# The softmax's 1e-9 added on GpSimd instead of VectorE, and two pairs of one-element VectorE operations joined

## The chip, the cores and the metric

One core of a Trainium2 chip runs the whole kernel. The metric is the device time of one execution in microseconds (us); smaller is better. In the profile PE is TensorE, DVE is VectorE, ACT is ScalarE, POOL is GpSimd and SP is SyncE.

## What is computed

A window attention with global tokens (4 batches, 8 heads, 512 local and 32 global positions, 64 elements a head, all float32), and behind it two feed-forward networks on the 2,176 rows that come out.

```python
def sm(s):
    s = s - np.max(s, axis=-1, keepdims=True)
    e = np.exp(s)
    return e / (np.sum(e, axis=-1, keepdims=True) + 1e-09)
out_g = sm(q_g @ [k_g, k_l].T / 8) @ [v_g, v_l]           # each global query sees all 544 keys
out_l = sm([q_l @ k_g.T / 8, where(|i-j|<=32, q_l @ k_l.T / 8, -1e9)]) @ [v_g, v_l]
x = (x @ w_in) * cos(x @ w_in) @ w_out                    # first network, 512 -> 2048 -> 512
y = relu(x @ w2_in)**2 @ w2_out                           # second network
```

## The kernel before

The attention is cut into 40 items. A **local item** is half of the queries of a pair of heads: four units `u`, each of 128 rows of scores with 160 keys (128 of the window, 32 global). There are 32 of them, numbered 0 to 31 here in the order in which they run. After each four local items comes a **global item** (8 in all), in which 128 rows of global queries see 544 keys.

The items run as a software pipeline. At step `s` a fixed list of stages (`CFG['order']`) is written out, each for the item that is `lag` steps behind; every engine works through its own instructions strictly in the order in which they are written, and waits at an instruction until what it needs is there. The stages that matter here, in the order of one step:

- `S`: PE computes the scores into PSUM (L400, for a global item L526).
- `KC`: POOL copies parts of the transposed keys (L333, L335, L343).
- `CC`: POOL finishes a piece of a weight's conversion (L163). `BG` and `CB` are more such background work for the networks, put on POOL, DVE or ACT by a table of room per step: L142, L172, L185, L724 on POOL, L151, L156, L172, L185, L724 on DVE.
- `SM` (item s): for each unit DVE adds the mask and finds the maximum (L416, two rows each in the profile); ACT takes the exponential and sums the row (L426). For a global item DVE finds two maxima (L541), joins them (L546), scales by -0.125 (L547), and ACT takes the exponentials (L551).
- `RC` (item s-1): DVE adds 1e-9 to the four sums in the small tile `st` (L440), then takes the reciprocal (L443). For a global item DVE adds two sums (L565), adds 1e-9 (L568), takes the reciprocal (L571).
- `NM` (item s-1): POOL scales the global-key part into `pg` (L448) and units 1 to 3 (L455); DVE scales unit 0 (L455). For a global item POOL scales all of `ptg` (L575).
- `OE`: DVE or ACT copies a finished output out of PSUM (L509, L613).
- `TM`, `TE`, `OM` in later steps: PE transposes the scaled weights (L468, L469; L583 for a global item), ACT copies them (L474, L478), PE multiplies with the values (L484, L496, L602).

Behind the attention come the steps of the two networks, ordered by a planner; their first matmuls (L850) stand in PE's queue between the last of the attention. The planner has nothing to do with the stages above.

Of the kernel before, what the change touches and what calls it, by code (L numbers as in the profile page):

```python
# [16 lines left out]
ALU = mybir.AluOpType  # L17
# [35 lines left out]
def kernel(  # L53
# [14 lines left out]
    nc = tc.nc  # L68
# [319 lines left out]
    class Local:  # L388
# [20 lines left out]
        def softmax(self):  # L409
            self.pt = lp.tile([P, 4, KTB], F32, tag="pt", name="pt", bufs=4)  # L410
            self.st = lp.tile([P, 3, 4], F32, tag="st", name="st", bufs=4)

            def unit(u):
                i = 2 * self.hb + u % 2
                m = masks[1] if i == 0 else masks[2] if i == 3 else masks[0]
                nc.vector.tensor_tensor_reduce(  # L416
                    out=self.pt[:, u, :],
                    in0=self.s[u // 2][:, 160 * (u % 2) : 160 * (u % 2) + 160],
                    in1=m,
                    scale=-0.125,  # L420
                    scalar=3.0e38,
                    op0=ALU.add,
                    op1=ALU.min,
                    accum_out=self.st[:, 0, u : u + 1],
                )
                nc.scalar.activation(  # L426
                    self.pt[:, u, :],
                    self.pt[:, u, :],
                    AF.Exp,
                    bias=self.st[:, 0, u : u + 1],  # L430
                    scale=-1.0,
                    accum_out=self.st[:, 1, u : u + 1],
                )

            return [lambda u=u: unit(u) for u in range(4)]

        def recip(self):
            st = self.st
            return [
                lambda: nc.vector.tensor_scalar(  # L440
                    st[:, 2, :], st[:, 1, :], 1e-9, None, op0=ALU.add
                ),
                lambda: nc.vector.reciprocal(st[:, 2, :], st[:, 2, :]),  # L443
            ]
# [69 lines left out]
    class Global:  # L514
# [19 lines left out]
        def softmax(self):  # L534
            self.pt = lp.tile([P, 544], F32, tag="ptg", name="ptg", bufs=1)
            self.st = lp.tile([P, 8], F32, tag="stg", name="stg", bufs=2)
            st = self.st
            n = (320, 224)

            def top(i):  # L540
                nc.vector.tensor_reduce(  # L541
                    st[:, i : i + 1], self.s[i][:, 0 : n[i]], op=ALU.max, axis=AX.X
                )

            def rest():
                nc.vector.tensor_tensor(st[:, 2:3], st[:, 0:1], st[:, 1:2], op=ALU.max)  # L546
                nc.vector.tensor_scalar(  # L547
                    st[:, 2:3], st[:, 2:3], -0.125, None, op0=ALU.mult
                )
                for i in range(2):  # L550
                    nc.scalar.activation(  # L551
                        self.pt[:, 320 * i : 320 * i + n[i]],
                        self.s[i][:, 0 : n[i]],
                        AF.Exp,
                        bias=st[:, 2:3],
                        scale=0.125,
                        accum_out=st[:, 4 + i : 5 + i],
                    )

            return [lambda: top(0), lambda: top(1), rest]  # L560

        def recip(self):
            st = self.st
            return [
                lambda: nc.vector.tensor_tensor(  # L565
                    st[:, 6:7], st[:, 4:5], st[:, 5:6], op=ALU.add
                ),
                lambda: nc.vector.tensor_scalar(  # L568
                    st[:, 6:7], st[:, 6:7], 1e-9, None, op0=ALU.add
                ),  # L570
                lambda: nc.vector.reciprocal(st[:, 6:7], st[:, 6:7]),  # L571
            ]
# [903 lines left out]
```

## Time and profile before

| | |
|---|---|
| time, median of 3 runs | 875.22 us (874.52 to 875.74) |
| time of the profiled execution | 873.37 us, its span 871.5 us |
| busy share of the span | PE 98%, DVE 75%, ACT 61%, POOL 67% |
| attention, and networks behind it | to about 148 us; from there to the end |

The profiled execution's own time is 1.9 us above its span, and 1.85 us below the median of the runs. A busy share is a mean over stages that differ: in the attention four engines are nearly full, behind it PE is. The profile counts an instruction as busy from its start to its end, also while it is held up inside; what an engine waits for ahead of an instruction is shown as idle time.

### The profile page before, as it was taken

The numbers are of one execution on the slowest core, as the hardware profiler recorded it, in microseconds if no ns is written. First come the engines' busy times: TensorE is split into PE (matmuls) and PEld (weight loads), VectorE is DVE, ScalarE is ACT, GpSimd is POOL, SyncE is SP. The second block draws the span as 40 slices with busy tenths as digits, with TensorE's granted clock in tenths as the row PEclk, the third lists the DMA queues.
The fourth block names the chain that finished last, engine by engine and source line by source line (L and its number), as shares of the span: only waits on it lengthen the run. The fifth ranks groups of instructions, "written<-read, shape, count | busy, mean of one in ns | idle before, by whom it ended". The sixth has DMA issues, their size and how long they took to land.

```text
span 871.5 us, 17134 instructions
## 1 busy us (share of the span) xinstructions
PE 849.9 (98%) x6028; PEld 783.9 (90%) x6028; DVE 656.7 (75%) x1409; ACT 531.5 (61%) x1275; POOL 583.5 (67%) x666
## 2 busy tenths in 40 slices
PE   7889999999999999999999999999999999999998
PEld 5668777999999999999999998889888989898886
DVE  6589997899798777967788898896756767454544
ACT  5679887987776656666555867655544554342331
POOL 6479998899887564758358899985645647432221
PEclk9999999999999999999999999999999999999999
DMA  7899664547774577557727547566764687346633
GB/s 164 201 205 206 136 209 140 229 177 252 286 291 176 192 303 271 168 171 302 278 73 260 216 171 266 195 229 235 276 209 141 242 297 222 131 166 248 214 119 85
DMA packets 134261, 182.00 MB, mean 209 GB/s; under 512 B 60960, under 2 KB 114720, under 8 KB 134176
## 3 DMA queue, kind: packets, MB, share of 16 engines
q1 hardware_dynamic: 130736, 179.79, 62.6%
q10 hardware_dynamic: 3440, 1.11, 0.5%
q8 instruction: 48, 0.79, 0.4%
q14 instruction: 37, 0.30, 0.1%
HBM read 141.03 MB, written 35.65 MB: 203 GB/s over the span
## 4 chain that ended last, share of the span: by engine, by line
PE 82%; DVE 6%; POOL 4%; ACT 2%; DMA 2%; issue 1%; SPq 1%; POOLq 0%; ACTq 0%
PE y L942 41%; PE hb L850 16%; PE ha L850 10%; PE he L850 10%; DVE pt L416 1%; POOL xs L172 1%; ACT pt L426 1%; PE s L400 1%; PE o L484 1%; POOL g L172 1%; DMA kn<-in_k_l_dram 1%; PE o L496 1%; POOL xr L724 1%; PE og L602 1%; POOL wf L163 1%
## 5 line engine op out<-in xcount | busy, mean ns | idle before, releaser
L172 POOL TENSOR_TENSOR g<-cr,g 128x384 fp32r<-128x384 f32 (+1 forms) x192 | 203.8, 1074 | 144.9 <-ACT g L901 139.4
L953 DVE TENSOR_TENSOR xt<-y,xt 128x384 f32<-128x384 f32 (+2 forms) x287 | 170.5, 596 | 96.2 <-PE y L942 94.5
L942 PE MATMUL y<-g,wo 128*128 128x384 f32 (+1 forms) x1152 | 219.1, 327 | 0.5 <-DVE xt L953 0.4
L942 PE MATMUL y<-wo,g 128*128 128x512 f32 x816 | 209.4, 393 | 0.0
L942 PEld LDWEIGHTS y<-g,wo 128*128 128x128 f32 x1152 | 193.9, 188 | 1.6 <-ACT wo L205 0.7
L942 PEld LDWEIGHTS y<-wo,g 128*128 128x128 f32 x816 | 150.0, 188 | 24.1
L850 PE MATMUL hb<-xs,wi 128*128 128x384 f32 (+1 forms) x864 | 167.3, 328 | 1.4 <-ACT cr L890 1.2
L850 PEld LDWEIGHTS hb<-xs,wi 128*128 128x128 f32 x864 | 147.7, 189 | 7.6 <-ACT cr L890 1.6
L850 PE MATMUL he<-xs,wi 128*128 128x384 f32 (+1 forms) x576 | 111.4, 328 | 1.4 <-DVE he L864 0.8
L850 PE MATMUL ha<-xs,wi 128*128 128x384 f32 (+1 forms) x576 | 111.2, 328 | 0.5 <-ACT ptg L551 0.5
L901 ACT ACTIVATE g<-cr 128x384 fp32r<-128x384 f32 (+1 forms) x192 | 93.9, 502 | 20.3 <-DVE cr L893 19.4
L163 POOL TENSOR_TENSOR wf<-wf,cc 128x512 uint32<-128x512 uint32 x64 | 87.8, 1376 | 24.9 <-DVE wf L151 18.2
L850 PEld LDWEIGHTS he<-xs,wi 128*128 128x128 f32 x576 | 98.2, 188 | 5.9 <-DVE cr L893 1.2
L850 PEld LDWEIGHTS ha<-xs,wi 128*128 128x128 f32 x576 | 97.9, 188 | 3.3 <-ACT ptg L551 0.8
L887 ACT ACTIVATE cr<-cr,halfpi 128x384 f32<-128x384 f32 (+1 forms) x96 | 56.0, 594 | 9.9 <-DVE cr L882 8.6
L156 DVE SCALAR_TENSOR_TENSOR cc<-raw,cc 128x512 uint32<-128x512 uint32 x64 | 61.9, 973 | 0.0
L426 ACT ACTIVATE pt<-pt,st 128x160 f32<-128x160 f32 x128 | 53.2, 423 | 2.7 <-DVE st L416 2.4
L147 ACT ACTIVATE cc<-raw 128x512 uint32<-128x512 uint32 x64 | 42.4, 670 | 20.3 <-DMA raw<-in_moe_w_out_dram 9.0
L151 DVE TENSOR_SCALAR wf<-wf 128x512 uint32<-128x512 uint32 x64 | 49.3, 775 | 4.3 <-POOL wf L142 3.2
L858 ACT ACTIVATE s<-hb 128x384 f32<-128x384 f32 (+1 forms) x48 | 22.7, 473 | 48.8 <-PE hb L850 48.7
L858 ACT ACTIVATE s<-he 128x384 f32<-128x384 f32 (+1 forms) x48 | 22.6, 472 | 32.5 <-PE he L850 32.4
L172 POOL TENSOR_TENSOR wi<-ws,wi 128x512 fp32r<-128x512 f32 x23 | 30.8, 1342 | 15.9 <-ACT wi L196 12.3
(147 smaller groups left out, 1338.4 us busy)
## 6 DMA issues: line engine op xcount, KB each, us to landing
xs<-xs_T SPq DMA_DIRECT2D x48, 768.0 KB, 5.9
xs<-xs_B SPq DMA_DIRECT2D x36, 768.0 KB, 5.5
raw<-in_moe_w_in_dram SPq DMA_DIRECT2D x32, 512.0 KB, 5.3
raw<-in_moe_w_out_dram SPq DMA_DIRECT2D x32, 512.0 KB, 4.5
xs<-xs_T SPq DMA_DIRECT2D x24, 640.0 KB, 5.5
xs_T<-xs SPq DMA_DIRECT2D x16, 768.0 KB, 4.3
xs<-xs_B SPq DMA_DIRECT2D x18, 640.0 KB, 5.3
xs_B<-xs SPq DMA_DIRECT2D x12, 768.0 KB, 4.9
```

The costliest lines, as they stand in the source:

```text
L147: A.activation(v, raw[q, m, c][:, :, 0].bitcast(U32), AF.Copy, scale=2.0**-29)
L151: V.tensor_scalar(u, u, 3, None, op0=ALU.logical_shift_left)
L156: V.scalar_tensor_tensor(v, t[:, :, 1].bitcast(U32), 0x80000000, v, op0=ALU.bitwise_and, op1=ALU.bitwise_or,)
L163: G.tensor_tensor(u, u, v, op=ALU.add)
L172: eng.tensor_tensor(lo, x, hi.bitcast(F32), op=ALU.subtract)
L426: nc.scalar.activation(self.pt[:, u, :], self.pt[:, u, :], AF.Exp, bias=self.st[:, 0, u : u + 1], scale=-1.0, accum_out=self.st[:, 1, u : ...
L850: nc.tensor.matmul(out, lhsT=w[:, ws, c : c + P], rhs=xs[:, xh, kk, 0:n], start=start and k == 0, stop=k == 5, skip_group_check=True,)
L858: A.activation(self.sb[name], self.hold(bank_name), AF.Copy)
L887: A.activation(self.r[key], self.r[key], AF.Sin, bias=halfpi, scale=TWOPI)
L901: A.activation(GT[s, f][0][:, th * n : th * n + n], self.r[key], AF.Copy)
L942: nc.tensor.matmul(o, lhsT=l, rhs=r, start=k == 0, stop=k == 5)
L953: V.tensor_tensor(dst, y, dst, op=ALU.add)
```

## The change

The 1e-9 of the 32 local items goes from a DVE instruction to a POOL instruction on the same four numbers per partition; the reciprocal stays on DVE. In the 8 global items the maximum and the factor become one DVE instruction, and so do the sum and the 1e-9. What is computed stays the same.

```diff
         def recip(self):                       # local item
             st = self.st
             return [
-                lambda: nc.vector.tensor_scalar(
-                    st[:, 2, :], st[:, 1, :], 1e-9, None, op0=ALU.add
+                lambda: nc.gpsimd.tensor_scalar(
+                    st[:, 2, :], st[:, 1, :], 1e-9, 1.0, op0=ALU.add, op1=ALU.mult
                 ),
                 lambda: nc.vector.reciprocal(st[:, 2, :], st[:, 2, :]),
             ]
             def rest():                        # global item, softmax
-                nc.vector.tensor_tensor(st[:, 2:3], st[:, 0:1], st[:, 1:2], op=ALU.max)
                 nc.vector.tensor_scalar(
-                    st[:, 2:3], st[:, 2:3], -0.125, None, op0=ALU.mult
+                    st[:, 2:3], st[:, 0:1], st[:, 1:2], -0.125, op0=ALU.max, op1=ALU.mult
                 )
         def recip(self):                       # global item
             return [
-                lambda: nc.vector.tensor_tensor(
-                    st[:, 6:7], st[:, 4:5], st[:, 5:6], op=ALU.add
-                ),
                 lambda: nc.vector.tensor_scalar(
-                    st[:, 6:7], st[:, 6:7], 1e-9, None, op0=ALU.add
+                    st[:, 6:7], st[:, 4:5], st[:, 5:6], 1e-9, op0=ALU.add, op1=ALU.add
                 ),
                 lambda: nc.vector.reciprocal(st[:, 6:7], st[:, 6:7]),
             ]
```

How it moves instructions is seen in each engine's order. First DVE's, where a global item's softmax meets a local item's reciprocal (`stg` and `sg` belong to the global item, `st` and `pt` to the local one; behind each row the engines that it waits for). Before:

```order
L541 TENSOR_REDUCE stg<-sg 128x1 [waits PE_49] x2
L546 TENSOR_TENSOR stg<-stg 128x1 [waits DVE_49]
L547 TENSOR_SCALAR stg<-stg 128x1 [waits DVE_49]
L440 TENSOR_SCALAR st<-st 128x4 [waits Activation_49]
L443 RECIPROCAL st<-st 128x4 [waits DVE_49]
L455 TENSOR_SCALAR pt<-pt,st 128x128 [waits DVE_49]
L509 COPY xt<-o 128x256 [waits PE_49]
```

And in the changed kernel, at the same place:

```order
L541 TENSOR_REDUCE stg<-sg 128x1 [waits PE_49] x2
L546 TENSOR_SCALAR stg<-stg 128x1 [waits DVE_49]
L443 RECIPROCAL st<-st 128x4 [waits Pool_49]
L455 TENSOR_SCALAR pt<-pt,st 128x128 [waits DVE_49,Activation_49]
L509 COPY xt<-o 128x256 [waits PE_49]
```

Two rows are gone, and the reciprocal L443, which waited for DVE's own add, now waits for POOL.

Then POOL's queue from the key copies of one step to the scaling of local item 19 (`wf` and `cc` are background work on a weight). Before:

```order
L343 TENSOR_SCALAR kT<-ktail 128x64
L163 TENSOR_TENSOR wf_1569<-wf_1569,cc 128x512 [waits DVE_49]
L448 TENSOR_TENSOR pg<-pt,st 128x128 [waits PE_49,DVE_49,Activation_49,Pool_49]
L455 TENSOR_SCALAR pt<-pt,st 128x128 x3
L142 TENSOR_SCALAR wf_1569<-raw 128x512 [waits DMAHW1_49]
L448 TENSOR_TENSOR pg<-pt,st 128x128 [waits PE_49,DVE_49,Activation_49,Pool_49]
L455 TENSOR_SCALAR pt<-pt,st 128x128 x3
```

And in the changed kernel:

```order
L343 TENSOR_SCALAR kT<-ktail 128x64
L163 TENSOR_TENSOR wf_1561<-wf_1561,cc 128x512 [waits DVE_49]
L440 TENSOR_SCALAR st<-st 128x4 [waits Activation_49]
L448 TENSOR_TENSOR pg<-pt,st 128x128 [waits DVE_49,PE_49]
L455 TENSOR_SCALAR pt<-pt,st 128x128 x3
L142 TENSOR_SCALAR wf_1561<-raw 128x512 [waits DMAHW1_49]
L440 TENSOR_SCALAR st<-st 128x4 [waits Activation_49]
L448 TENSOR_TENSOR pg<-pt,st 128x128 [waits DVE_49,PE_49]
L455 TENSOR_SCALAR pt<-pt,st 128x128 x3
```

The add L440 stands directly ahead of the item's first scaling L448, behind all the copies and background work that POOL has ahead of it; L448 still waits for DVE, whose reciprocal now waits for L440. The orders of PE, ACT and SP are the same as before. In the changed kernel's file the lines behind L546 have numbers that are lower by 1 to 4.

## Rows read from the trace of the kernel before

**Rows 1.** The page's list of busy time: us, share of the span, instructions.

```profile
PE 849.9 (98%) x6028; PEld 783.9 (90%) x6028; DVE 656.7 (75%) x1409; ACT 531.5 (61%) x1275; POOL 583.5 (67%) x666
```

**Rows 2.** Busy time by stretch: stretch, its length, then each engine, TensorE's granted clock.

```profile
66.90:141.70 74.80, 72.43 (x1157) 57.83 (x1156) 71.76 (x292) 66.86 (x244) 68.92 (x130) 1.00 0.65 162
141.70:148.60 6.90, 6.39 (x76) 5.67 (x75) 4.54 (x11) 3.74 (x9) 6.90 (x9) 1.00 0.85 305
148.60:871.00 722.40, 715.41 (x4030) 675.86 (x4028) 533.97 (x898) 416.67 (x859) 465.70 (x432) 1.00 0.61 215
```

**Rows 3.** Two long pieces of the chain of waits, 74 to 125 us: start, duration.

```profile
75.81 1.06 DVE st L440
...
90.15 1.27 POOL wf L163
```

**Rows 4.** POOL's groups of instructions, 66.9 to 141.7: busy, mean | idle before, released by.

```profile
L455 POOL TENSOR_SCALAR pt<-pt,st 128x128 f32<-128x128 f32 x58 | 25.8, 458 | 0.0
L448 POOL TENSOR_TENSOR pg<-pt,st 128x128 f32<-128x128 f32 x20 | 8.1, 404 | 5.9 <-DVE st L443 4.6 <-PE tw L468 0.4 <-ACT ptg L551 0.4
...
L343 POOL TENSOR_SCALAR kT<-ktail 128x64 f32<-128x64 f32 x8 | 3.4, 426 | 0.0
```

**Rows 5.** DVE's groups of instructions, 66.9 to 141.7 us.

```profile
L440 DVE TENSOR_SCALAR st<-st 128x4 f32<-128x4 f32 x19 | 8.8, 462 | 0.0
...
L546 DVE TENSOR_TENSOR stg<-stg 128x1 f32<-128x1 f32 x5 | 2.2, 443 | 0.2
```

**Rows 6.** Local item 18, timelines of POOL and then DVE: start, duration, instruction.

```profile
91.39 0.39 POOL L448 TENSOR_TENSOR pg<-pt,st 128x128 f32<-128x128 f32 x1
...
88.69 0.18 DVE L443 RECIPROCAL st<-st 128x4 f32<-128x4 f32 x1
```

**Rows 7.** Local item 20, timelines of POOL and then DVE.

```profile
98.39 1.28 POOL L163 TENSOR_TENSOR wf<-wf,cc 128x512 uint32<-128x512 uint32 x1
100.08 0.41 POOL L448 TENSOR_TENSOR pg<-pt,st 128x128 f32<-128x128 f32 x1 [0.41 <-DVE st L443]
100.47 1.37 POOL L455 TENSOR_SCALAR pt<-pt,st 128x128 f32<-128x128 f32 x3
...
98.48 1.21 DVE L440 TENSOR_SCALAR st<-st 128x4 f32<-128x4 f32 x1
99.73 0.18 DVE L443 RECIPROCAL st<-st 128x4 f32<-128x4 f32 x1
```

**Rows 8.** From local item 16 to 17, timelines of DVE and then POOL.

```profile
82.48 0.18 DVE L443 RECIPROCAL st<-st 128x4 f32<-128x4 f32 x1
...
84.95 0.16 DVE L440 TENSOR_SCALAR st<-st 128x4 f32<-128x4 f32 x1
...
83.02 0.42 POOL L448 TENSOR_TENSOR pg<-pt,st 128x128 f32<-128x128 f32 x1
83.40 1.26 POOL L455 TENSOR_SCALAR pt<-pt,st 128x128 f32<-128x128 f32 x3
```

**Rows 9.** POOL lines L343 and L333, least/median/largest ns; a memset and three L455.

```profile
L343 POOL TENSOR_SCALAR kT<-ktail x16: 238/244/742, 9.8 to 129.8; 128x64 f32<-128x64 f32 x16
L333 POOL TENSOR_SCALAR kT<-kT x15: 557/562/575, 8.9 to 128.6; 128x448 f32<-128x448 f32 x15
...
0.27 0.10 POOL L1458 MEMSET const-float32-1.0<- 128x1 f32 x1
...
18.07 1.07 POOL L455 TENSOR_SCALAR pt<-pt,st 128x128 f32<-128x128 f32 x3
```

**Rows 10.** Timeline: a DVE instruction that waits for a POOL instruction alone.

```profile
59.12 0.64 POOL L142 TENSOR_SCALAR wf<-raw 128x512 f32<-128x512 f32 x1 [2.70 <-DMA raw<-in_moe_w_out_dram]
...
59.79 0.61 DVE L151 TENSOR_SCALAR wf<-wf 128x512 uint32<-128x512 uint32 x1 [2.27 <-POOL wf L142]
```

**Rows 11.** End of the attention, timelines of POOL and PE.

```profile
146.89 0.72 POOL L575 TENSOR_SCALAR ptg<-ptg,stg 128x544 f32<-128x544 f32 x1
...
147.67 0.66 PE L583 MATMUL twg<-ident,ptg 128*128 128x128 f32 x4 [0.51 <-POOL ptg L575]
```

## The prediction, made before the changed kernel ran

> **What bounds the kernel now.** First the list of busy time [rows 1]: PE has work for 98% of the span, so the kernel seems to be PE's, but that is a mean. The busy time by stretch [rows 2] shows two kinds of stage. From 148.6 us to the end PE stands idle for 722.40 - 715.41 = 7.0 us in all: whatever shifts the start of that stage shifts the end by nearly as much. The change lies wholly ahead of it. From 66.9 to 141.7 us, where local items 12 to 31 are normalised, PE, DVE, ACT and POOL are busy for 72.4, 71.8, 66.9 and 68.9 of 74.8 us: nothing has much room. The chain of waits between 74 and 125 us [rows 3] has DVE's add L440 among its longest pieces, and POOL's L163 too: it changes over between the two engines.
>
> POOL's groups [rows 4] show what the sum below is built on. POOL's 5.9 us of idle time in this stretch (74.80 - 68.92 in rows 2) all stand ahead of one line, the 20 instructions L448. So POOL is a chain of its own: each stop that is added to its queue moves its end, unless it falls into those 5.9 us. At the end of the attention PE stands for 0.51 us until POOL's L575 is through [rows 11]; from there POOL's delay is PE's.
>
> How the two engines meet in L440 is seen in item 20 [rows 7]. L440 on four elements takes 0.16 us when nothing disturbs it [rows 8], here 1.21: it begins at 98.48 and ends at 99.69, just when POOL's L163 ends (99.67). It is held until the instruction that POOL has begun is over. Then comes the reciprocal, and POOL's L448 0.17 us behind that one's end (99.91 to 100.08). POOL stood for 0.41 us.
>
> **What the change does, step by step.** Before, POOL needed DVE's reciprocal once an item. Now DVE's reciprocal needs POOL's add, which stands in POOL's queue behind its key copies and background work, and POOL's L448, the next in that queue, needs the reciprocal: a way there and back in every local item.
>
> The price of one such way when POOL comes last:
> - The add on POOL. No row has four elements. L343 and L333 have 64 and 448 and take at least 0.238 and 0.557 us [rows 9]: 0.00083 us an element, and so 0.19 us for four. Bounds: 0.10 us, a memset of one element, from below, and 0.43, L343's mean in this stretch [rows 4], from above. I take 0.19, as an undisturbed tensor_scalar is the nearest thing.
> - POOL to DVE: L151 starts 0.03 us after L142 ends (59.76 to 59.79) [rows 10].
> - The reciprocal: 0.18 us, and 0.17 us from its end to L448 [rows 7].
>
> Together 0.19 + 0.03 + 0.18 + 0.17 = 0.57 us an item that POOL doesn't spend on its other work. The 20 items of the stretch make 11.4 us. What POOL stood for there before, 5.9 us, is not paid twice: **+5.5 us**.
>
> The 20 items are of three sorts. In 9 there is no idle time ahead of L448, because POOL is late and DVE has long been done: in item 18 the reciprocal was through at 88.87, and L448 began at 91.39 [rows 6]. These pay the full 0.57. DVE loses more there, since its reciprocal, and behind it its own scaling L455, the copy out of PSUM and the next item's mask and maxima, wait for POOL's add: from 88.69 to about 91.6. In 7, like item 20, POOL stood for 0.41 us, and the rest is 0.16. In 4 DVE was really late, and POOL stood for what is left of the 5.9 us, some 0.75 an item; these pay nothing by themselves.
>
> But DVE can no longer run ahead, so it comes late more often. With both tied at each reciprocal, an item takes as long as the slower of the two. Behind item 16's reciprocal DVE had 84.95 - 82.48 = 2.47 us of work before the next add was due; POOL, from L448 at 83.02 to the end of L455 at 84.66, had 1.64, which with 0.17 and 0.18 ahead of it and its add and 0.03 behind it makes 2.21: DVE is late by 0.26. The same count over the 20 items finds three more (0.07, 0.19, 0.21): **+0.7 us**.
>
> What DVE saves lies beside this. L440 goes (8.8 us in 19 instructions, their holds included), and so does L546 (2.2 us in five), as the joined operation takes the place of L547 [rows 5]; the two operations of a global item's sum are the same case. It shortens DVE's way in items where DVE then waits for POOL's add anyway, so I cost it at nothing. If that cover were gone, POOL never being last, DVE's path would shorten by up to 8.8 + 2.2 = 11.0 us, of which ACT's 66.9 busy us of 74.8 would leave at most 7.9.
>
> Items 0 to 11 I also put at nothing: they run behind loads and PE, and one of their late adds, item 11, meets a 2.70 us wait of POOL for a DMA just ahead of it [rows 10].
>
> Sum: 5.5 + 0.7 = **+6.2 us** on POOL's chain at its last item, and on PE behind it. The profiled execution would take 873.37 + 6.2 = 879.6 us. It lay 1.85 us below the median; on the median of 875.22 I predict **881.4 us**.
>
> The Trainium skill has a rule against this move: GPSIMD Engine Reference, Key points, says that for elementwise work VectorE is structurally about twice as fast. By that the add would take an estimated 2 x 0.16 = 0.32 us, and the sum would be 8.8 us. Rows 9 don't bear it out for tiles as small as this: 64 elements take 0.24 us on POOL.
>
> **The rivals.**
> - *The add is held on POOL as well.* POOL's L343 takes 0.24 us undisturbed, but 0.43 on average in this stretch [rows 4, 9]; I take the difference for holds by DVE's background work on the other side, as in item 20 the other way round. If the add were held like that, each of 20 would cost 0.24 more: +4.8, 886.2 us. For it: DVE runs such background work in most items. Against it: where POOL comes last DVE stands at the reciprocal, and where DVE comes last it works on L416, with its scores in PSUM, and the add is early. The Trainium skill, SBUF — State Buffer, Who interferes with whom, says that whichever of the two engines starts first keeps the shared port pair for its whole instruction. The holds in rows 7 agree; it speaks for this rival only if DVE has such an instruction running when the add starts.
> - *POOL's own holds go, and it is faster.* POOL's instructions in this stretch contain holds: L455 averages 0.458 us over 58, where three undisturbed ones take 1.07 together, 0.36 each; L343 averages 0.426 for 0.24 [rows 4, 9]. If DVE, standing at the reciprocal, no longer got in the way, POOL would shed 58 x 0.098 + 8 x 0.186 = 7.2 us. That exceeds 6.2 by 1.0; and where POOL is then no longer late, in up to 9 items, L440's undisturbed 0.16 us counts on DVE's path, 1.4 more: 875.2 - 2.4 = 872.8 us. It decides from the point at which POOL sheds over 0.31 us an item. Against it: DVE's background work comes right behind the reciprocal, just when POOL runs L455; in item 20, where the engines already go in step, three L455 took 1.37 us [rows 7], three times the mean.
> - *Nothing is seen.* The delay could be taken up between 141.7 and 148.6 us, or by PE's 7.0 us of idle time behind it. Against it: POOL is busy for all 6.90 us of that short stretch [rows 2], and PE's later idle time is spread over 722 us: 875 us.
>
> **How the numbers follow.** A change of 0.2%, 1.75 us, is about what a measurement of this kernel can tell from none. My forecast, slower by 3 to 9 us, has 0.66: its lower end is the add at 0.10 us (20 x 0.09 = 1.8 less, and some of POOL's holds gone), its upper end the add at 0.3. The held add has 0.12, the faster kernel 0.12, no change within 1.75 us 0.10. Slower therefore has 0.78, the same 0.10, faster 0.12. A range of 874.2 to 886.2 us leaves out most of the faster case and half of the held add, about 2 in 10.
>
> **What would show it.** Right: in the profile after, POOL's idle time ahead of L448 is 0.38 us in nearly all late items and sums to 8 or more in items 12 to 31; DVE stands ahead of L443 for 15 us or more, waiting for POOL's L440; L440 on POOL takes about 0.19 us; the joined operations take 0.15; PE's L583 for the last global item starts at about 153.9 instead of 147.67. Wrong: L583 starts at 148 or earlier, or POOL's busy time for its old instructions from item 12 to 31 falls by 5 us or more, or the attention ends late and the networks' stage is shorter by as much.

## The result

| | before | changed | ratio, 95% interval |
|---|---|---|---|
| median time | 875.18 us (4 runs) | 883.07 us (4 runs) | 1.0096 (1.0082 to 1.0111) |
| profiled execution: time, span | 873.37, 871.5 us | 882.44, 880.7 us | |

The changed kernel is slower by 7.9 us by the medians. In the profiles the spans differ by 9.2 us, as the profiled execution of before lay 1.8 us below this median and that of the changed kernel 0.6 below its own.

The page's list of busy time of the changed kernel, as in [rows 1]:

```profile
PE 855.6 (97%) x6028; PEld 786.7 (89%) x6028; DVE 642.9 (73%) x1361; ACT 531.0 (60%) x1275; POOL 591.8 (67%) x698
```

DVE is busy for 13.8 us less than before and POOL for 8.3 more. Busy time by stretch, as in [rows 2]; the first stretch is again that of local items 12 to 31:

```profile
67.40:150.90 83.50, 76.50 (x1145) 59.26 (x1142) 61.03 (x265) 66.17 (x240) 73.59 (x149) 0.98 0.59 147
150.90:157.80 6.90, 6.02 (x74) 5.31 (x73) 4.61 (x11) 3.70 (x9) 6.90 (x9) 1.00 0.83 291
157.80:880.00 722.20, 715.33 (x4030) 676.04 (x4028) 534.24 (x898) 416.39 (x859) 466.51 (x433) 1.00 0.61 215
```

Behind the attention nothing has changed: 722.2 us with 715.3 of PE, as before. The whole difference lies ahead of it. From item 12 to 31 TensorE's granted clock was 1.00 before and is 0.98 on average now; that comes back with dve_more below. The stretch of the 20 items has grown by 8.7 us, and in it POOL now stands idle for 9.9 us and DVE for 22.5, where it was 5.9 and 3.0 [rows 2]. What they stand for is seen in all instructions of three lines (least, median and largest ns), and who waits for them:

```profile
L440 POOL TENSOR_SCALAR st<-st x32: 192/193/194, 11.3 to 149.9; 128x4 f32<-128x4 f32 x32
...
who waited for it (us, times):
  DVE st L443: 24.1, 21
...
L443 DVE RECIPROCAL st<-st x32: 167/177/179, 11.6 to 150.1; 128x4 f32<-128x4 f32 x32
...
who waited for it (us, times):
  POOL pg L448: 12.0, 23
...
L546 DVE TENSOR_SCALAR stg<-stg x8: 214/214/216, 19.0 to 148.8; 128x1 f32<-128x1 f32 x8
```

The add on POOL takes 0.193 us in every one of 32 cases. DVE waits 21 times for it, 24.1 us in all, and POOL in its turn waits 23 times for the reciprocal. Local item 18 in the timelines of POOL and then DVE, as in [rows 6]:

```profile
92.57 1.27 POOL L163 TENSOR_TENSOR wf<-wf,cc 128x512 uint32<-128x512 uint32 x1
93.92 0.19 POOL L440 TENSOR_SCALAR st<-st 128x4 f32<-128x4 f32 x1
94.47 0.40 POOL L448 TENSOR_TENSOR pg<-pt,st 128x128 f32<-128x128 f32 x1 [0.36 <-DVE st L443]
94.86 1.57 POOL L455 TENSOR_SCALAR pt<-pt,st 128x128 f32<-128x128 f32 x3
...
91.24 0.08 DVE L416 DVE_READ_ACCUMULATOR2_ANT st<- 128x1 f32 x1
94.15 0.18 DVE L443 RECIPROCAL st<-st 128x4 f32<-128x4 f32 x1 [2.82 <-POOL st L440]
94.43 0.52 DVE L455 TENSOR_SCALAR pt<-pt,st 128x128 f32<-128x128 f32 x1
```

DVE is through with the next item's maxima at 91.32 and stands for 2.82 us until POOL has worked off its copies and L163. Then POOL does the add, stands for 0.36, and only then goes on. From the end of L163 (93.84) to L448 (94.47) POOL spends 0.63 us. The end of the attention, timeline of PE, as in [rows 11] (L583 is L579 in this file):

```profile
156.90 0.66 PE L579 MATMUL twg<-ident,ptg 128*128 128x128 f32 x4 [0.88 <-POOL ptg L571]
```

It starts 9.2 us later than before, which is the difference of the spans.

### The profile page after: what moved, and what is told of

The parts are those of the page before. It is cut to its first block, busy times and chain, and to the rows that moved or that the text cites. A ratio compares the mean times of both kernels' runs of the same rounds, so it can differ in the third digit from the quotient of the medians.

```text
span 880.7 us, 17121 instructions
## 1 busy us (share of the span) xinstructions
PE 855.6 (97%) x6028; PEld 786.7 (89%) x6028; DVE 642.9 (73%) x1361; ACT 531.0 (60%) x1275; POOL 591.8 (67%) x698
## 4 chain that ended last, share of the span: by engine, by line
PE 82%; POOL 9%; DVE 3%; DMA 2%; ACT 2%; issue 1%; SPq 1%; POOLq 0%; DVEq 0%; ACTq 0%
PE y L938 40%; PE hb L846 16%; PE ha L846 10%; PE he L846 10%; POOL pt L455 2%; POOL xs L172 1%; PE s L400 1%; PE o L484 1%; POOL g L172 1%; PE tk L295 1%; PE o L496 1%; POOL wi L172 1%; POOL xr L720 1%; DMA raw<-in_moe_w_out_dram 1%; POOL pg L448 1%
## 5 line engine op out<-in xcount | busy, mean ns | idle before, releaser
L172 POOL TENSOR_TENSOR g<-cr,g 128x384 fp32r<-128x384 f32 (+1 forms) x192 | 204.2, 1076 | 144.7 <-ACT g L897 139.8
L938 PEld LDWEIGHTS y<-wo,g 128*128 128x128 f32 x816 | 150.0, 188 | 24.1
L163 POOL TENSOR_TENSOR wf<-wf,cc 128x512 uint32<-128x512 uint32 x64 | 87.7, 1375 | 23.9 <-DVE wf L151 18.2
L156 DVE SCALAR_TENSOR_TENSOR cc<-raw,cc 128x512 uint32<-128x512 uint32 x64 | 61.6, 968 | 0.1
L151 DVE TENSOR_SCALAR wf<-wf 128x512 uint32<-128x512 uint32 x64 | 48.2, 756 | 0.4 <-ACT wf L140 0.3
L455 POOL TENSOR_SCALAR pt<-pt,st 128x128 f32<-128x128 f32 x96 | 43.6, 468 | 0.0
```

The lines of the kernel that those rows point to most:

```text
L151: V.tensor_scalar(u, u, 3, None, op0=ALU.logical_shift_left)
L156: V.scalar_tensor_tensor(v, t[:, :, 1].bitcast(U32), 0x80000000, v, op0=ALU.bitwise_and, op1=ALU.bitwise_or,)
L163: G.tensor_tensor(u, u, v, op=ALU.add)
L172: eng.tensor_tensor(lo, x, hi.bitcast(F32), op=ALU.subtract)
L455: (nc.vector if u < CFG["ndv"] else nc.gpsimd).tensor_scalar(self.pt[:, u, 0:P], self.pt[:, u, 0:P], self.st[:, 2, u : u + 1], 1.0, op0=AL ...
L938: nc.tensor.matmul(o, lhsT=l, rhs=r, start=k == 0, stop=k == 5)
```

## The experiments

Runs of one kernel scatter: the 23 runs of before beside local_only lie between 871.54 and 876.69 us. In the 13 profiles item 12 starts anywhere from 66.0 to 69.5 us, and there the granted clock differs: ahead of that item it stood at 0.50 (1.2 GHz) for 3.4 us in before, for 10.2 in reduce_join, which starts it last. Whether that is all of the scatter isn't shown. So beside each time stands the length of the stretch, from the start of POOL's first scaling of local item 12 (`pg`, L448) to that of item 31 in the profile of the run. It is 74.2 us before and 82.4 with the change; each is from one profile. The ratios are to the kernel before, run beside each kernel.

| run | median, us | ratio, 95% interval | items 12 to 31, us |
|---|---|---|---|
| local_only | 883.66 | 1.0105 (1.0080 to 1.0129) | 82.8 |
| global_only | 874.18 | 0.9992 (0.9977 to 1.0008) | 74.3 |
| no_wait | 875.27 | 1.0011 (0.9997 to 1.0025) | 75.7 |
| no_add | 871.58 | 0.9970 (0.9950 to 0.9990) | 71.4 |
| pool_twice | 883.43 | 1.0105 (1.0090 to 1.0120) | 82.5 |
| dve_more | 881.06 | 1.0080 (1.0061 to 1.0099) | 80.9 |
| odd_add | 873.50 | 0.9998 (0.9983 to 1.0013) | 74.4 |
| odd_join | 874.74 | 1.0003 (0.9991 to 1.0015) | 73.9 |
| early_add | 881.75 | 1.0087 (1.0071 to 1.0103) | 80.3 |
| act_add | 873.94 | 0.9993 (0.9981 to 1.0004) | 73.5 |
| reduce_join | 872.29 | 0.9977 (0.9967 to 0.9987) | 72.3 |

Theory A is the prediction's: the way from DVE to POOL and back, paid in POOL's queue. Its rivals are in the expectations.

### Which half of the change it is

**local_only**: the kernel before with the first hunk of the change alone. 

> The add of 1e-9 for the local items on POOL, the global items as before. Theory A (the way from DVE to POOL and back in each local item, paid in POOL's queue): all of the loss stays, 882 to 884 us, POOL idle ahead of L448 plus ahead of L440 about 9 us in items 12 to 31. Theory B (part of the loss comes from the joined global operations, which take 0.21 us each where 0.15 was expected): under 881 us.

**global_only**: the kernel before with the other two hunks alone. 

> The joined operations in the global items alone, the local add on DVE as before. Theory A: 872 to 875.5 us, since two operations that are held behind POOL go from DVE's path. Theory B: over 876 us.

All of the loss is in the local add, and the joined operations alone change nothing that can be measured. B falls: they take 0.21 us where L547 took 0.154, but that isn't seen in the time.

### The wait or the work

**no_wait**: POOL's instructions stay, the reciprocal doesn't wait for them.

```diff
                 lambda: nc.gpsimd.tensor_scalar(
-                    st[:, 2, :], st[:, 1, :], 1e-9, 1.0, op0=ALU.add, op1=ALU.mult
+                    self.sx, st[:, 1, :], 1e-9, 1.0, op0=ALU.add, op1=ALU.mult
                 ),
-                lambda: nc.vector.reciprocal(st[:, 2, :], st[:, 2, :]),
+                lambda: nc.vector.reciprocal(st[:, 2, :], st[:, 1, :]),
```

> As the changed kernel, but POOL's add of the 32 local items writes to a tile that nothing reads, and DVE takes the reciprocal of the bare sums: the 1e-9 of the local items doesn't reach the result. POOL's instructions and their order are those of the changed kernel, only the reciprocal's wait for POOL is gone. Theory A: DVE stands no longer ahead of L443, POOL's idle time ahead of L448 falls to under 4 us in items 12 to 31, 871 to 876 us. Theory C (POOL is simply given more work, and the wait is incidental): 880 us or more.

**no_add**: the same without the first of the two operations.

```diff
-                lambda: nc.gpsimd.tensor_scalar(
-                    st[:, 2, :], st[:, 1, :], 1e-9, 1.0, op0=ALU.add, op1=ALU.mult
-                ),
-                lambda: nc.vector.reciprocal(st[:, 2, :], st[:, 2, :]),
+                lambda: nc.vector.reciprocal(st[:, 2, :], st[:, 1, :]),
```

> As the changed kernel without any add for the local items (their 1e-9 is left out). It shows what taking L440 from DVE is worth when nothing is put in its place. Theory A: the holds of L440 and POOL's stops of 0.41 us behind them go, 868 to 872 us; against the run before it in this list, whose POOL has 32 adds of 0.19 us more, lower by 2 to 4 us, because POOL's queue passes its work on one to one. If POOL were not the chain, the two would be within 1 us.

With the wait gone and POOL's 32 adds still there, the time is that of before: C falls. POOL's groups from 67 to 145 us in no_wait (its lines are one higher; `sx` is the add):

```profile
L456 POOL TENSOR_SCALAR pt<-pt,st 128x128 f32<-128x128 f32 x58 | 22.1, 396 | 0.0
L449 POOL TENSOR_TENSOR pg<-pt,st 128x128 f32<-128x128 f32 x20 | 8.6, 429 | 2.4 <-DVE st L444 1.1
L441 POOL TENSOR_SCALAR sx<-st 128x4 f32<-128x4 f32 x20 | 7.4, 369 | 1.6
```

The idle time ahead of the scaling has fallen to 2.4 us. The add itself now averages 0.369 us, where it took 0.193 in each case of the changed kernel: with DVE running on beside it, POOL's add is held too, as one of the rivals had it. In 11 of the 20 items it takes 0.377 to 0.697 us, each time while DVE runs one of its background instructions (L151, L156, L172 or L721), and in the other nine 0.193. In the changed kernel the wait keeps these out of its way. Without the adds the time is 3.7 us lower, within the 2 to 4 us expected, and the stretch 4.3 us shorter: POOL's queue passes its work on. So the change can be taken apart by medians: taking L440 from DVE, with the joined operations, gives about 3 us (no_add against before), the adds on POOL take them back (3.7, no_add to no_wait), and the wait costs the rest, 7.8 us (no_wait to the changed kernel, measured in different series). These 7.8 us hold all that the wait brings with it, among it a second wait of L455 and a stretch at a lower clock (both below).

### Which engine has room

**pool_twice** doubles POOL's add, into a tile that nothing reads; **dve_more** puts a DVE operation ahead of the reciprocal.

```diff
+                lambda: nc.gpsimd.tensor_scalar(                      # pool_twice
+                    self.sx, st[:, 1, :], 1e-9, 1.0, op0=ALU.add, op1=ALU.mult
+                ),
...
+                lambda: nc.vector.tensor_scalar(                      # dve_more
+                    self.sx, st[:, 1, 0:1], 1e-9, None, op0=ALU.add
+                ),
                 lambda: nc.vector.reciprocal(st[:, 2, :], st[:, 2, :]),
```

> The changed kernel with a second add of the same size on POOL right behind the first in each local item, into a tile that nothing reads. Theory A (POOL's queue is the chain of the attention): 20 items from 12 to 31 by 0.16 us, 3 us more than the changed kernel, 885.5 to 887 us, less where the second add lies beside the reciprocal on DVE: as that takes 0.18 us and the way back 0.14, the second add fits wholly into POOL's idle time ahead of L448, and then the time stays at 883 us while that idle time shrinks by 0.16 an item. If any work added to POOL costs in full, 886 us or more.

> The changed kernel with one more DVE operation (one element, 0.15 us, into a tile that nothing reads) directly ahead of each local reciprocal. Theory A: DVE stands there for POOL's add in 17 of 20 late items, so it is hidden: 882.5 to 884 us. Theory D (DVE is still what bounds the attention): 32 by 0.19, 886 us or more.

Both are hidden, as theory A has it. POOL's groups in pool_twice from 67.5 to 151.4 us:

```profile
L452 POOL TENSOR_TENSOR pg<-pt,st 128x128 f32<-128x128 f32 x20 | 8.0, 399 | 1.8
L441 POOL TENSOR_SCALAR st<-st 128x4 f32<-128x4 f32 x20 | 3.9, 193 | 1.7
L444 POOL TENSOR_SCALAR sx<-st 128x4 f32<-128x4 f32 x20 | 3.9, 193 | 1.6
```

The idle time ahead of `pg` is 1.8 us, where the changed kernel has 7.3 (below): the second add lies where POOL stood for the reciprocal. What the way there and back costs POOL is time in which it could do something else, if there were something in its queue. D falls as well, but dve_more does better than hidden: 881.06 us, 2 us under the changed kernel, with intervals that overlap; its stretch is 1.5 us shorter. One part of that is in the groups of DVE and POOL. In the changed kernel, 67.4 to 150.9 us:

```profile
L455 DVE TENSOR_SCALAR pt<-pt,st 128x128 f32<-128x128 f32 x20 | 10.5, 524 | 2.1
...
L443 DVE RECIPROCAL st<-st 128x4 f32<-128x4 f32 x20 | 3.5, 177 | 20.8 <-POOL st L440 20.7
...
L455 POOL TENSOR_SCALAR pt<-pt,st 128x128 f32<-128x128 f32 x58 | 27.7, 490 | 0.0
L448 POOL TENSOR_TENSOR pg<-pt,st 128x128 f32<-128x128 f32 x20 | 8.0, 399 | 7.3 <-DVE st L443 5.5 <-PE tw L468 0.8 <-PE s L400 0.7
L440 POOL TENSOR_SCALAR st<-st 128x4 f32<-128x4 f32 x20 | 3.9, 193 | 1.7
```

and in dve_more, 68.4 to 150.4 (L455 is L459 here, L448 is L452):

```profile
L459 DVE TENSOR_SCALAR pt<-pt,st 128x128 f32<-128x128 f32 x20 | 5.7, 287 | 0.7
L447 DVE RECIPROCAL st<-st 128x4 f32<-128x4 f32 x20 | 3.5, 176 | 19.7 <-POOL st L441 19.5
...
L459 POOL TENSOR_SCALAR pt<-pt,st 128x128 f32<-128x128 f32 x58 | 26.3, 465 | 0.0
L452 POOL TENSOR_TENSOR pg<-pt,st 128x128 f32<-128x128 f32 x20 | 8.6, 430 | 7.3 <-DVE st L447 5.4 <-PE tw L472 0.4 <-PE tlg L586 0.4
```

DVE's own scaling L455 takes 0.524 us in the changed kernel and 0.287 here. The order of the change shows why: there L455 waits for DVE and ACT, `[waits DVE_49,Activation_49]`, since the add that used to wait for ACT ahead of it has gone; in dve_more the extra operation does that waiting, and L455 waits for DVE alone (each of the 32 in the changed kernel has a semaphore instruction of DVE's queue ahead of it, in dve_more none has). In the timeline above L455 starts 0.28 us after the reciprocal (94.15 to 94.43), 0.04 us ahead of POOL's `pg`, and ends just behind it; with one wait it starts at 0.21 and is through in 0.29. That 0.07 us decides this is read from the two profiles and not tested by itself.

It is the smaller part of the 1.5 us. From one L448 to the next the changed kernel takes at most 0.06 us longer than dve_more, 0.7 us in 18 steps; in one step, from item 19 to 20, it takes 7.55 us against 6.73. There TensorE's granted clock differs. The stretch in the changed kernel, as in [rows 2], and then timelines of PE, DVE and POOL:

```profile
96.03:99.44 3.41, 3.08 (x22) 2.75 (x25) 2.58 (x8) 1.93 (x6) 2.97 (x9) 0.50 0.14 31
96.36 1.12 PE L295 MATMUL tk<-ident,kn 128*128 128x128 f32 x4 [2.40 <-DVE qT L356]
98.47 1.32 PE L400 MATMUL s<-kT,qT 64*64 64x160 f32 x16
99.84 0.33 DVE L416 CUSTOM_DVE_ANT_0 pt<-s,mask 128x160 f32<-128x160 f32 x1 [0.98 <-PE s L400]
101.40 1.00 POOL L571 TENSOR_SCALAR ptg<-ptg,stg 128x544 f32<-128x544 f32 x1 [0.91 <-ACT pt L426]
```

and in dve_more, where the clock stayed at 1.00:

```profile
97.02 0.66 PE L295 MATMUL tk<-ident,kn 128*128 128x128 f32 x4 [2.23 <-DVE qT L356]
99.68 0.33 DVE L417 CUSTOM_DVE_ANT_0 pt<-s,mask 128x160 f32<-128x160 f32 x1 [0.21 <-PE s L400]
101.25 1.07 POOL L575 TENSOR_SCALAR ptg<-ptg,stg 128x544 f32<-128x544 f32 x1
```

At 0.50 (1.2 GHz) the four transposes of L295 take 1.12 us instead of 0.66. The scores come late, DVE waits 0.98 us for them instead of 0.21, its reciprocal of the global item (L567, 101.07 to 101.23) follows, and POOL stands 0.91 us ahead of L571, which starts 0.17 us behind that reciprocal (the row names ACT as the last that it waited for). In dve_more POOL doesn't stand there. Before the clock fell, at 96.03, PE had stood idle since 93.96, waiting for DVE. The profiles of local_only, pool_twice and early_add have such a stretch of 3.4 us at 0.50 at the same place; those of before and the other seven runs have none from item 12 to 31. Why dve_more has none, though PE stands 2.23 us there, isn't shown.

**early_add**: the changed kernel with POOL's add at the head of the step.

```diff
-                lambda: nc.gpsimd.tensor_scalar(                      # in recip
-                    st[:, 2, :], st[:, 1, :], 1e-9, 1.0, op0=ALU.add, op1=ALU.mult
-                ),
...
+        e = it(s - L["RC"])
+        if isinstance(e, Local):
+            e.early()                       # the add on POOL, ahead of all stages of the step
         for c in CFG["order"]:
```

> The changed kernel with POOL's add moved within its own queue: at the head of the next step, ahead of that step's background work (L163, L142) and not behind it. In 8 of the items 12 to 31 such work stood directly ahead of the add. Theory A: there the reciprocal is done while POOL still works, 8 by 0.33 us for the way back and DVE's stand shorter, minus what POOL now waits for ACT's sums: 876 to 881 us. If the place in the queue were of no account and only the add's work counted: 883 us.

It is 881.75 us, just above the expected range; its interval overlaps that of the changed kernel, and its stretch is 2.1 us shorter. Item 18 in its timelines, POOL and then DVE (the add is L445, the reciprocal L440, `pg` L451):

```profile
92.36 0.19 POOL L445 TENSOR_SCALAR st<-st 128x4 f32<-128x4 f32 x1
92.64 1.27 POOL L163 TENSOR_TENSOR wf<-wf,cc 128x512 uint32<-128x512 uint32 x1
93.87 0.40 POOL L451 TENSOR_TENSOR pg<-pt,st 128x128 f32<-128x128 f32 x1
...
92.59 0.18 DVE L440 RECIPROCAL st<-st 128x4 f32<-128x4 f32 x1 [1.59 <-POOL st L445]
92.88 1.12 DVE L458 TENSOR_SCALAR pt<-pt,st 128x128 f32<-128x128 f32 x1
```

POOL no longer stands ahead of `pg` in this item, since L163 lies over the reciprocal. But DVE still waits 1.59 us for the copies that stand ahead of the add, and its scaling is then held for most of L163. The place in the queue seems to count, for less than half of what was hoped.

### A better place for the add

**odd_add** and **odd_join**: the add on DVE over five elements, without and with the joined operations.

```diff
-            self.st = lp.tile([P, 3, 4], F32, tag="st", name="st", bufs=4)
+            self.st = lp.tile([P, 13], F32, tag="st", name="st", bufs=4)
...
-                    st[:, 2, :], st[:, 1, :], 1e-9, None, op0=ALU.add
+                    st[:, 8:13], st[:, 3:8], 1e-9, None, op0=ALU.add
```

> The kernel before with the local add still on DVE, but on five elements instead of four (the fifth is a maximum, its result isn't read). An odd number of elements should keep the operation out of the mode in which it is held behind POOL's instruction. If the holds of L440 come from that mode: L440 takes about 0.16 us everywhere, POOL's stops of 0.41 us shrink, 870 to 873 us. If the holds have another cause: L440 as before up to 1.3 us, 875 us.

> The five-element local add on DVE together with the joined operations in the global items: all of the 1e-9 in the result, and nothing of the softmax's sum on POOL. Theory A with the hold by the mode: lower than either alone, 868 to 872 us, near the kernel that leaves the local add out. Otherwise as the kernel with the joined operations alone.

Both miss: the time doesn't change. The five-element add is held just as long, as all its instructions show:

```profile
L440 DVE TENSOR_SCALAR st<-st x32: 158/168/1333, 11.7 to 142.2; 128x5 f32<-128x5 f32 x32
```

An odd count alone doesn't free the operation from being held. That agrees with the Trainium skill, VectorE: DVE Perf Modes, What auto-detection actually checks: for the two-port mode 2×_2P, the expectation's "mode", it has the condition that the outermost non-unit dimensions of source and destination are both even *or equal*, and five and five are equal.

**act_add**: the add on ACT, behind the item's exponentials, with the joined operations.

```diff
+            def add():
+                nc.scalar.activation(self.st[:, 2, :], self.st[:, 1, :], AF.Copy, bias=1e-9)
-            return [lambda u=u: unit(u) for u in range(4)]
+            return [lambda u=u: unit(u) for u in range(4)] + [add]
...
-                lambda: nc.gpsimd.tensor_scalar(                      # in recip
-                    st[:, 2, :], st[:, 1, :], 1e-9, 1.0, op0=ALU.add, op1=ALU.mult
-                ),
```

> The add of the local items on ACT, directly behind the item's four exponentials, with the joined operations in the global items. Neither DVE nor POOL has the add, and no engine waits for POOL. Theory A: as without the add, if ACT has room for 20 by about 0.2 us in the 8 us that it is free from item 12 to 31: 870 to 874 us. If ACT has no room: 875 to 878 us. If any move of the add off DVE cost as POOL's did: over 880 us.

No loss here, though the add has left DVE just as well: what costs is POOL's place, not the move. Nor is there a gain, 0.9993: ACT's 20 adds take 4.1 us between 60 and 146 us.

```profile
L436 ACT ACTIVATE st<-st 128x4 f32<-128x4 f32 x20 | 4.1, 206 | 0.6
```

**reduce_join**: the add on DVE as a reduction over pairs, with the joined operations. The four small tiles are kept for the whole attention, with 1e-9 in every second place.

```diff
+    ST = [lp.tile([P, 16], F32, name=f"st{i}") for i in range(4)]
+    for t in ST:
+        nc.vector.memset(t[:, 4:12], 1e-9)
...
-                    accum_out=self.st[:, 1, u : u + 1],
+                    accum_out=self.st[:, 4 + 2 * u : 5 + 2 * u],
...
-                lambda: nc.vector.tensor_scalar(
-                    st[:, 2, :], st[:, 1, :], 1e-9, None, op0=ALU.add
+                lambda: nc.vector.tensor_reduce(
+                    st[:, 12:16], st[:, 4:12].rearrange("p (u two) -> p u two", two=2),
+                    op=ALU.add, axis=AX.X,
...
```

> The local add on DVE as a tensor_reduce over pairs (a sum, and a 1e-9 that is written into the small tile once at the start), with the joined operations in the global items. The reductions L541 are never held behind POOL in any profile here, so this add takes about 0.17 us without holds: 870 to 873.5 us, between the kernel without the add and the one with the joined operations alone. If the holds of L440 were only DVE's waiting for what it would wait for anyway: 874 to 875 us.

```profile
L441 DVE TENSOR_REDUCE st<-st x32: 150/156/164, 11.5 to 141.2; 128x4 f32<-128x8 f32 x32
```

None of its 32 adds is held, where the largest hold of L440 was over a microsecond. It computes all of the softmax and beats both kernels, by little: 872.29 us, 0.9977 (0.9967 to 0.9987) of the time before.

## Why the prediction was right, and where it was off

The side, the place and the mechanism were right: 883.07 us lies in the range of 874.2 to 886.2, and POOL's queue is where it is paid. Of the signs named in the prediction three came out otherwise: POOL's idle time ahead of L448 sums to 7.3 us and not to 8, the joined operations take 0.21 us and not 0.15, and L583 starts at 156.90 and not at about 153.9. By its steps:

- **One way there and back.** Forecast 0.57 us an item, measured 0.63 to 0.64. The add was given 0.19 and takes 0.193; POOL to DVE 0.03, measured 0.04 in item 18; reciprocal and way back 0.35, measured 0.32. Missing in the sum was POOL's stop ahead of the add itself, 0.08 us (93.84 to 93.92), 1.7 us in 20 items.
- **What POOL stood for before.** Rightly set off: the new idle time ahead of L448 is 7.3 us and doesn't come on top of the old 5.9.
- **DVE late in four more items, +0.7 us.** Wrong: in the profile DVE stands for POOL's add in 18 of the 20 items, in one of them for 0.11 us only. It comes late in two, items 17 and 21, where POOL stands for 0.41 us instead of 0.36: 0.1 us in all. The way's 0.06 us more an item, 1.2 in all, hides that: two misses of opposite sign, which is luck.
- **What DVE saves, at nothing.** Right for the change: DVE stands for 20.7 us at the reciprocal, and the joined operations alone give 0.9992. Where the cover is gone, in no_add, L440 is worth about 3 us.
- **The step that was mis-sized.** The sum was 6.2 us; the medians say 7.9, the profiled stretch 8.2. From item 12's L448 to item 31's POOL has the same instructions in both profiles, so its 8.2 us can be split. The adds are 3.7, the stops ahead of them 1.6, and the stops ahead of L448 go from 5.9 to 7.0: that is what the sum was about, 6.4 us over 19 items, where 6.2 was forecast over 20. The other two have no term in it. One is the 0.9 us that POOL stands ahead of L571, behind the stretch at the lower clock. The other, 1.0 us, is that POOL's old instructions take longer: L455 1.8 in all (0.458 us on average before [rows 4], now 0.490), L448, L333 and L571 0.2 to 0.3 each, less 1.3 for L343 and 0.3 for L335. DVE's L455 went from 0.392 us on average before to 0.524; its second wait stood in the order that was quoted, and got no price. Items 0 to 11 were put at nothing. Item 12 starts 0.9 us later in the profile, 0.6 of it that item's own; the rest is within the scatter of that start.
- **The held add.** It doesn't happen in the changed kernel, for the reason given: where POOL comes last, DVE stands. no_wait shows that it would happen otherwise.
- **POOL's own holds go.** Some do: L343 averages 0.259 us, in the 20 items, after 0.426. L455 took that back.

```profile
L343 POOL TENSOR_SCALAR kT<-ktail 128x64 f32<-128x64 f32 x8 | 2.1, 259 | 0.0
```

What stays open is why the clock fell in the changed kernel and not in dve_more, and whether it does so in every execution: each kernel has one profile.

## What to carry to other kernels

An operation on four numbers costs its engine 0.2 us, but a value that goes from engine A to B and back to A costs what stands ahead of it in B's queue as well, and keeps A from running ahead: look at where B is when A needs the value, not at how long the operation takes. Before taking an operation off a busy engine, ask whether its time is work or a hold; a hold may go if the operation takes another form on the same engine. And an instruction that is removed may have done a wait for the one behind it, which then starts later and loses its turn. Where two kernels differ by a little, set them side by side step by step before naming one cause: here over half of 1.5 us stood in one step of 19.

## What the runs showed of the hardware that was not expected

- A DVE add over four or five elements was held behind a POOL instruction for up to 1.3 us, a reduction over eight never (0.150 to 0.164 us in 32 cases).
- POOL's add of four elements took 0.193 us in all 32 cases of the changed kernel, where DVE stood still or ran L416, L541 or L546. In no_wait it took 0.377 to 0.697 us in the 11 of items 12 to 31 in which DVE ran one of its background instructions.
- A DVE scaling that waited for two engines' signals started 0.28 us after the reciprocal's start, with one signal 0.21 us, and ran for 0.524 us, with POOL's `pg` beside it, against 0.287.
- The joined one-element operation L546, with a second operand from a tile and a constant, took 0.214 us, where L547, with a constant alone, took 0.154.
- TensorE's granted clock stood at 0.50 (1.2 GHz) for 3.4 us in the middle of the attention in four of the 13 profiles. The four transposes of L295 took 1.12 us there, and 0.66 at 1.00 (2.4 GHz).
